# The first nine tiles' instruction list written anew in finer pieces, with 13 of 21 warming products taken out

## The chip, the cores and the metric

One core of a Trainium2 chip runs the whole kernel. The metric is device microseconds (us) of one execution; "before" has three runs: 471.3, 472.75 and 474.21, median 472.75.

## The reference

```python
# attention within chunks of 64 tokens: q, k, v are 8 x 8 x 576 x 64 (batch, heads, tokens, width)
scores = (1 / sqrt(64)) * q_c @ k_c.T
attn = exp(scores - max); attn = attn / (sum(attn) + 1e-9)
x = (attn @ v_c), heads side by side            # 4608 x 512
# SoLU feed-forward
h = x @ w_in                                    # 4608 x 1024
e = exp(h - max(h)); solu = h * e / (sum(e) + 1e-9)
ln = (solu - mean) / sqrt(var + 1e-6) * g_ln
out = ln @ w_out                                # 4608 x 512
```

The two weights arrive as 64-bit floats; the kernel reads their two 32-bit words.

## The kernel before

The 4608 tokens are 36 tiles of 128. A tile holds two chunks of 64 tokens with all eight heads. For each tile: scores (q against k), softmax, values (attn against v, the result is x transposed), the first layer into ph (128 x 1024), SoLU and normalisation into z, z turned so that its 1024 features lie on the partitions, and the second layer into po (128 x 512). The products of the two layers run in fp32r, and each operand is split into a high part and a remainder, so that three products stand for one: x_h with wi_l, x_h with wi_h, x_l with wi_h, and the same with z and wo. The first layer is 24 products of 128 x 512 (two column halves n, four row blocks cc, three pairs m), the second 24 in three thirds of eight.

TensorE (PE) does all products and some transposes. VectorE (DVE) and ScalarE (ACT) read the PSUM results. GpSimd (POOL) does small work and issues DMAs, SyncE (SP) issues most DMAs. Each engine runs its instructions strictly in the order in which the program lists them, and waits where an operand or a buffer is missing (class Order, line 40).

The work of tiles 0 to 4 and the preparation of tiles 5 to 8 stand in the string START (lines 18 to 31), word by word; each word starts a step or, if it has been begun, takes it one `yield` further (lines 750 to 768). From tile 5 on, a loop (line 775) lists the work. The words that matter here:

- n loads q and k of a tile as they lie in memory, v loads v, P loads a pair of row blocks of a weight (0 to 3 of w_in, 4 to 7 of w_out), g loads g_ln, Q and q load a batch's q and k in 32-wide strips. All of these stand in SP's queue.
- N transposes q (N:i:0) or k (N:i:1) on PE into a PSUM bank (named tp; there are two, and nat and s_e transposes, z transposes and g share them), then evicts it to qT or kT on ACT, or on DVE if the word is in MOVED (lines 34 to 37).
- c clips the high words of a weight pair (POOL, tile w_a, two buffers) and then scales them on ACT (the "prelude", w_a from w_a). b makes bits of the low words (tile w_b, DVE, or POOL if MOVED says so). C joins both on DVE. t makes the high part on ACT (wi_h or wo_h), d the remainder on DVE (wi_l or wo_l).
- S scores; A the softmax's maximum and subtraction on DVE, then the exponential on ACT; B its sum, reciprocal and product on DVE (s_e); T transposes s_e on PE and copies it to attn_t on ACT in four pieces. From tile 6 on, U turns it on DVE instead (a_b), and eight DMAs, four from SP and four from POOL, bring it to attn_t.
- V values on PE, then x_h on ACT and x_l on DVE. M first layer. X maximum (h_nmax, DVE) and exponential (ACT). Y multiplies by ph (DVE) and scales the result on ACT or POOL. R squares on ACT and a power on POOL. z turns z by PE transposes (tiles 0 and 1), Z on DVE with 16 DMAs z_t from z_b (tiles 2 and up). F one third of a second layer. o scales po into o_sb, O stores it. K turns a later tile's q and k on DVE.
- w is a product of the identity with itself into ph that nobody reads (warm, line 742); w:3 stands for three.

Of the ph tiles only tile 1's has its own PSUM place (PH2); tiles 0, 2, 3, 4 and so on follow each other in one buffer, so a tile's first product waits until DVE has multiplied the one before (Y). The loop's first values, of tiles 6 and 7, read what the eight attn_t DMAs bring. When the START list is through, the order of the loop is the same for every pair of tiles.

ffn_in (line 489) fixes the order of the 24 products; for tile 0 it sorts them by row block and yields after every six, for others it sorts by half and puts x_l last, in one piece.

Of the kernel before, what the change touches and what calls it, by code (L numbers as in the profile page):

```python
# [15 lines left out]


START = """
n:0 w:3 N:0:0 N:0:0 w:1 N:0:1 N:0:1 g w:1 S:0 A:0 G P:0 P:0 n:1 A:0 c:0 c:0 w:3 N:1:0 N:1:0 w:1
N:1:1 b:0 N:1:1 G P:1 w:1 S:1 B:0 v:0 C:0 A:1 t:0 T:0 T:0 c:1 c:1 w:4 V:0 V:0 P:2 b:1 c:2 n:2  # L20
d:0 P:3 A:1 n:3 w:6 N:2:0 w:1 N:2:1 C:1 V:0 B:1 t:1 c:2 T:1 N:2:0 b:2 N:2:1 T:1 d:1 S:2 n:4
M:0 M:0 C:2 t:2 c:3 c:3 v:1 A:2 A:2 b:3 d:2 C:3 N:3:0 N:3:1 N:3:1 M:0 N:3:0 S:3 N:4:0 B:2 N:4:1
t:3 N:4:0 A:3 P:5 d:3 c:5 N:4:1 A:3 T:2 T:2 S:4 V:1 M:0 P:4 n:5 B:3 T:3 V:1 V:1 M:1 X:0 X:0 T:3
A:4 A:4 b:4 v:2 N:5:1 c:4 n:6 P:7 c:5 N:5:0 c:4 Y:0 Y:0 n:7 N:5:1 V:2 b:5 v:3 B:4 N:5:0 V:2 b:7
C:4 z:0:1 P:6 v:5 N:6:0 X:1 v:4 C:5 N:6:0 S:5 Q:2 q:8 t:4 V:2 d:4 N:6:1 N:6:1 X:1 t:5 A:5 Y:1
M:2 z:0:1 z:0:1 X:2 A:5 R:0 z:0:0 z:0:0 q:8 N:7:1 q:8 c:6 S:6 Y:1 V:3 X:2 T:4 T:4 z:0:0 d:5 F
V:3 Y:2 Y:2 N:7:0 A:6 c:6 c:7 V:3 b:6 B:5 C:6 n:8 N:7:0 M:3 R:1 c:7 q:8 N:7:1 C:7 T:5 z:1:0 t:6
T:5 S:7 t:7 d:6 X:3 X:3 d:7 V:4 V:4 Y:3 Y:3 R:2 z:1:1 A:6 F F A:7 V:4 z:1:0 z:1:0 v:6 Z:2 A:7
M:4 F B:7 Z:3 o:0 V:5 z:1:1 z:1:1 B:6 F F v:7 O:0 X:4 N:8:0 X:4 U:6 U:7 V:5 Y:4 V:5 K:9 Y:4 N:8:0
R:4 R:3 N:8:1 N:8:1 o:1  # L30
"""


MOVED = """
N:0:0=dve N:8:0=dve N:8:1=dve Y:0=pool Y:1=pool Y:3=pool b:7=pool c:0=pool c:1=pool c:2=pool
c:3=pool c:4=pool c:5=pool c:6=pool c:7=pool
"""


# [23 lines left out]
def chunk_attention_then_solu_ffn(  # L63
# [18 lines left out]
    G = S // 32  # L82
# [24 lines left out]
    def po():  # L107
# [246 lines left out]
    def attn(i):  # L354
        return sy if order.on and i % 2 else sx
# [32 lines left out]

    def softmax_e(i):
        e = st[i, "e"]  # L390
        act.activation(e, e, AF.Exp, scale=SCALE)

    def softmax_b(i):
        e = st[i, "e"]
        ssum = small.tile([P, H], F32, name="s_sum")
        dve.tensor_reduce(out=ssum, in_=ES[i % 2], axis=AX.X, op=ALU.add)
        rinv = small.tile([P, H], F32, name="s_rinv")
        dve.reciprocal(out=rinv, in_=ssum)
        a = st[i, "e"] = work.tile([P, H, CH], F32, name="s_e") if i < PE_TURNED else e
# [66 lines left out]
        x_low(i)  # L466

    def start_softmax(i):
        softmax_a(i)
        yield  # L470
        softmax_e(i)

# [13 lines left out]
    def ffn_in(i):  # L486
        xh, xl = st[i, "x"]
        pool_h = ps_h2 if i in PH2 else ps_h
        ph = st[i, "h"] = pool_h.tile([P, 2, HALF], F32, name="ph")

        sums = [(n, cc, m) for n in range(2) for cc in range(NCC) for m in range(3)]
        if i == 0:
            sums.sort(key=lambda s: s[1])
        else:

            sums.sort(key=lambda s: (s[0], s[2] == 2))
        for at, (n, cc, m) in enumerate(sums):
            if i == 0 and at and at % 6 == 0:
                yield
            cols = slice(n * HALF, (n + 1) * HALF)  # L500
            x, w = ((xh, wi_l), (xh, wi_h), (xl, wi_h))[m]
            await_arrivals(pe.matmul(
                ph[:, n, :], x[:, cc, :], w[:, cc, cols],
                start=(cc == 0 and m == 0), stop=(cc == NCC - 1 and m == 2),
            ), at, i)
# [222 lines left out]
    first = 5  # L728
# [46 lines left out]
    for i in range(first, NT):  # L775
# [10 lines left out]
        if not odd:  # L786

            if i + 3 < NT:
                softmax_e(i + 3)
                softmax_b(i + 3)  # L790
                attn_turn(i + 3)
            if i + 1 < NT:
                x_high(i + 1)
# [17 lines left out]
        part()  # L811
        if odd:
            if i + 3 < NT:
                softmax_a(i + 3)
                softmax_e(i + 3)
            if i + 1 < NT:
                x_high(i + 1)
        elif i + 1 < NT:
            x_low(i + 1)
# [5 lines left out]
        if odd:  # L825
            if i + 1 < NT:
                x_low(i + 1)
            if i + 3 < NT:
                softmax_b(i + 3)
                attn_turn(i + 3)  # L830
        else:
            for m in (i + 4, i + 5):
                if m < NT:
                    turn(m)
# [8 lines left out]
            z_turn(i)  # L843
        store_rest()
        if odd and i + 4 < NT:
            softmax_a(i + 4)
    while queue:
        third_ahead()

# [31 lines left out]
```

## Time and profile before

| what | us |
|---|---|
| median of three runs | 472.75 |
| the profiled execution | 473.01 |
| its span, first to last instruction | 471.2 |
| PE busy | 461.9 |
| DVE busy | 374.1 |
| ACT busy | 256.4 |
| POOL busy | 147.6 |
| first product of a first layer (ph) starts | 22.39 |
| values of tile 6 start | 86.59 |

Times of rows count from the span's start. A timeline row gives start, duration, engine, line, operation, output<-input, shapes and count; in brackets stands how long the engine idled before it, and what ended that. All recorded operations have line 54, a helper, so groups are told apart by tiles and shapes. A product of 128 x 512 is shown with 0.39 us, but the next one starts 0.227 later, since they are pipelined. In windows, "x" counts records.

### The profile page before, as it was taken

The page shows a single profiled execution, that of the slowest core. Times are in us where ns is not written, and L with a number is a line of the kernel's source. Part 1 is how long each engine was busy: PE and PEld are TensorE (multiplying, and loading weights), DVE is VectorE, ACT ScalarE, POOL GpSimd, SP SyncE. Part 2 cuts the span into 40 slices and gives each one's busy share as a digit, 9 for nine tenths or more (in the row PEclk, how much of TensorE's full clock was granted, in tenths as well). Part 3 has the DMA queues.
Part 4 walks back from the last instruction along what each step waited for, and adds up shares of the span by engine and source line. Part 5 has one row for each costly group of instructions (what it writes and reads, how often), then busy time and mean ns, then how long its engine had stood idle before and what let it go on. Part 6 is the DMA issues. An engine that isn't in the chain of part 4 may idle for free.

```text
span 471.2 us, 11062 instructions
## 1 busy us (share of the span) xinstructions
PE 461.9 (98%) x4212; PEld 380.9 (81%) x4212; DVE 374.1 (79%) x521; ACT 256.4 (54%) x422; POOL 147.6 (31%) x298
## 2 busy tenths in 40 slices
PE   8999999999999999999999999999999999999997
PEld 6677778788888888888888888888888888888886
DVE  3999999797869887878788878797979797954441
ACT  2979984555544646464645455554555554545451
POOL 2212716151505050505050505042514141424430
PEclk9999999999999999999999999999999999999999
DMA  9999999878786878687258496948743535343231
GB/s 244 313 278 217 216 138 179 176 184 150 194 140 170 154 181 162 167 154 177 70 144 167 134 175 157 180 126 173 160 112 105 121 91 136 85 118 96 73 95 50
DMA packets 192924, 72.57 MB, mean 154 GB/s; under 512 B 177188, under 2 KB 177960, under 8 KB 191976
## 3 DMA queue, kind: packets, MB, share of 16 engines
q1 hardware_dynamic: 186200, 58.89, 57.3%
q0 software_dynamic: 6528, 12.86, 10.3%
q8 instruction: 33, 0.54, 0.5%
q14 instruction: 19, 0.16, 0.1%
q10 hardware_dynamic: 144, 0.13, 0.1%
HBM read 36.70 MB, written 9.44 MB: 98 GB/s over the span
## 4 chain that ended last, share of the span: by engine, by line
PE 85%; DMA 5%; DVE 3%; ACT 3%; SPq 2%; issue 1%; DVEq 0%; ACTq 0%
PE po L54 39%; PE ph L54 37%; PE tp L54 5%; PE sx L54 4%; SPq L54 2%; DMA nat<-in_q_dram 2%; DMA v_sb<-in_v_dram 2%; ACT z L54 1%; DMA attn_t<-a_b 1%; ACT attn_t L54 1%; ACT wo_h L54 1%; DVE z_b L54 1%; DVE z L54 0%; DVE s_sum L54 0%; ACT sq L54 0%
## 5 line engine op out<-in xcount | busy, mean ns | idle before, releaser
L54 ACT ACTIVATE z<-ph,h_nmax 128x1024 f32<-128x1024 f32 x36 | 40.2, 1118 | 139.1 <-DVE h_nmax L54 139.1
L54 PE MATMUL po<-wo_l,z_h 128*128 128x512 f32 (+1 forms) x288 | 113.0, 392 | 0.0
L54 PE MATMUL ph<-wi_l,x_h 128*128 128x512 f32 x288 | 112.8, 392 | 0.0
L54 PE MATMUL ph<-wi_h,x_h 128*128 128x512 f32 x288 | 112.2, 389 | 0.0
L54 PE MATMUL po<-wo_h,z_l 128*128 128x512 f32 (+1 forms) x288 | 111.6, 388 | 0.0
L54 PE MATMUL po<-wo_h,z_h 128*128 128x512 f32 (+1 forms) x288 | 111.4, 387 | 0.0
L54 POOL DMA_DIRECT2D z_t<-z_b x144 | 71.8, 506 | 27.0 <-DVE z_b L54 21.9
L54 PE MATMUL ph<-wi_h,x_l 128*128 128x512 f32 x288 | 78.1, 390 | 0.0
L54 POOL TENSOR_TENSOR u<-ssq,eps 128x1 f32<-128x1 f32 x36 | 6.8, 189 | 213.3 <-ACT sq L54 213.1
L54 DVE TENSOR_REDUCE h_nmax<-ph 128x1 f32<-128x1024 f32 x36 | 44.0, 1222 | 31.3 <-PE ph L54 31.2
L54 PEld LDWEIGHTS ph<-wi_h,x_l 128*128 128x128 f32 x288 | 53.9, 188 | 11.6 <-DVE x_l L54 0.4
L54 PEld LDWEIGHTS po<-wo_l,z_h 128*128 128x128 f32 x288 | 54.1, 188 | 11.4
L54 PEld LDWEIGHTS ph<-wi_l,x_h 128*128 128x128 f32 x288 | 54.1, 188 | 11.5 <-ACT x_h L54 0.2
L54 PEld LDWEIGHTS po<-wo_h,z_l 128*128 128x128 f32 x288 | 54.1, 188 | 11.1
L54 PEld LDWEIGHTS ph<-wi_h,x_h 128*128 128x128 f32 x288 | 54.1, 188 | 11.0
L54 PEld LDWEIGHTS po<-wo_h,z_h 128*128 128x128 f32 x288 | 54.1, 188 | 10.5
L54 DVE TENSOR_TENSOR z_l<-z_t,z_h 128x1024 fp32r<-128x1024 f32 (+1 forms) x37 | 42.0, 1136 | 20.9 <-ACT z_h L54 17.7
L54 DVE SCALAR_TENSOR_TENSOR z<-ph,z 128x1024 f32<-128x1024 f32 x36 | 44.1, 1224 | 13.3 <-ACT z L54 13.2
L54 ACT ACTIVATE z<-z,z_sum 128x1024 f32<-128x1024 f32 x33 | 38.1, 1155 | 22.9 <-DVE z L54 21.7
L54 DVE STREAM_TRANSPOSE z_b<-z 128x1024 f32<-128x1024 f32 x34 | 41.2, 1212 | 7.2 <-DMA v_sb<-in_v_dram 3.3
L54 ACT CAST z_h<-z_t 128x1024 fp32r<-128x1024 f32 (+1 forms) x37 | 36.0, 972 | 8.5 <-PE po L54 4.9
L54 ACT ACTIVATE o_sb<-po,r 128x512 f32<-128x512 f32 (+1 forms) x36 | 24.3, 674 | 24.7 <-POOL r L54 18.6
(76 smaller groups left out, 589.8 us busy)
## 6 DMA issues: line engine op xcount, KB each, us to landing
out_dram<-o_sb SPq DMA_DIRECT2D x35, 256.0 KB, 2.5
v_sb<-in_v_dram SPq DMA_DIRECT2D x32, 256.0 KB, 4.3
z_t<-z_b POOLq DMA_DIRECT2D x128, 64.0 KB, 2.8
z_t<-z_b SPq DMA_DIRECT2D x128, 64.0 KB, 3.0
q_st<-in_q_dram SPq DMA_DIRECT2D x96, 72.0 KB, 3.3
k_st<-in_k_dram SPq DMA_DIRECT2D x96, 72.0 KB, 3.1
w_raw<-in_moe_w_out_dram SPq DMA_DIRECT2D x4, 1024.0 KB, 7.5
attn_t<-a_b POOLq DMA_DIRECT2D x60, 64.0 KB, 3.8
```

Source lines behind the costliest of these rows:

```text
L54: ins = make(*args, **kwargs)
```

## The change

START lists the same work anew, MOVED sends other steps to other engines, and five functions yield in more places, so that the list can set their parts apart: the softmax's maximum, subtraction and exponential are three steps (A), its sum, reciprocal and product three (B); the two halves of a w_out pair's high part (t) and remainder (d) are two steps each; the first layer of tiles 0 to 4 comes in four pieces of six products (M). Tile 1's first layer is sorted by row block like tile 0's, and in both the two x_l products of a row block come last of its six. Warming products: 21 before (w:3 three times among them, w:4 and w:6), 8 now, all as w:1; none stands ahead of the first transposes, and five stand in a row behind the values of tile 0. The loop is as before.

```diff
 START = """
-n:0 w:3 N:0:0 N:0:0 w:1 N:0:1 N:0:1 g w:1 S:0 A:0 G P:0 P:0 n:1 A:0 c:0 c:0 w:3 N:1:0 N:1:0 w:1
+n:0 N:0:0 N:0:1 N:0:1 N:0:0 P:0 P:0 n:1 S:0 w:1 A:0 A:0 A:0 b:0 c:0 B:0 B:0 c:0 C:0 N:1:0 N:1:0
...
 MOVED = """
-N:0:0=dve N:8:0=dve N:8:1=dve Y:0=pool Y:1=pool Y:3=pool b:7=pool c:0=pool c:1=pool c:2=pool
-c:3=pool c:4=pool c:5=pool c:6=pool c:7=pool
+N:0:0=dve N:8:0=dve b:7=pool c:0=pool c:1=pool c:2=pool c:3=pool c:4=pool c:5=pool c:6=pool c:7=pool
+b:4=pool b:5=pool z:0:1=dve Y:2=pool
...
             for y in range(2):
+                if y:
+                    yield
                 g = g_sb[:, 2 * m + y:2 * m + y + 1]
                 act.activation(top[:, y], a[:, y], AF.Copy, scale=g)
...
         for y in range(2):
+            if y:
+                yield
             dve.scalar_tensor_tensor(
...
             out=nmax, in_=sv, axis=AX.X, op=ALU.max, negate=True
         )
+        yield
         e = ES[i % 2][:, :, :CH]
...
         dve.tensor_reduce(out=ssum, in_=ES[i % 2], axis=AX.X, op=ALU.add)
+        yield
         rinv = small.tile([P, H], F32, name="s_rinv")
         dve.reciprocal(out=rinv, in_=ssum)
+        yield
...
     def start_softmax(i):
-        softmax_a(i)
+        yield from softmax_a(i)
         yield
         softmax_e(i)
...
-        if i == 0:
-            sums.sort(key=lambda s: s[1])
+        if i < 2:
+            sums.sort(key=lambda s: (s[1], s[2] == 2))
         else:
             sums.sort(key=lambda s: (s[0], s[2] == 2))
         for at, (n, cc, m) in enumerate(sums):
-            if i == 0 and at and at % 6 == 0:
+            if i < first and at and at % 6 == 0:
                 yield
```

In the loop the calls of softmax_a and softmax_b become `whole(softmax_a(...))` and `whole(softmax_b(...))`, which run the parts without a break.

On POOL, from the sixth weight clip on: w_a is a clip, w_b are bits, z is a scaling of tile 0 or 1, u and r belong to tile 0's norm. Before, from the six clips of pairs 0 to 5:

```order
L54 TENSOR_SCALAR w_a<-w_raw 128x1024 x6
L54 TENSOR_SCALAR z<-z,z_sum 128x1024
L54 TENSOR_SCALAR w_b<-w_raw 128x1024
L54 TENSOR_TENSOR u<-ssq,eps 128x1
L54 TENSOR_TENSOR r<-u,mhalf 128x1
```

And now, from the clips of pairs 0 to 3 and 5:

```order
L55 TENSOR_SCALAR w_a<-w_raw 128x1024 x5
L55 TENSOR_SCALAR w_b<-w_raw 128x1024
L55 TENSOR_SCALAR w_a<-w_raw 128x1024
L55 TENSOR_SCALAR w_b<-w_raw 128x1024 x2
L55 TENSOR_SCALAR w_a<-w_raw 128x1024
L55 TENSOR_TENSOR u<-ssq,eps 128x1
```

The bits of pairs 5 and 4 have come from DVE, each behind its pair's clip; the bits of pair 7 stood on POOL before too, and pair 7's clip now comes right behind them.

On DVE, the last instructions of the list and the first of the loop: a_b turns the attention of tiles 6 (e0) and 7 (e1), the second-layer z is tile 4's. Before, from tile 4's maximum on:

```order
L54 TENSOR_REDUCE h_nmax_1076<-ph_975 128x1
L54 STREAM_TRANSPOSE a_b_1088<-e0_97 128x8x2x32
L54 STREAM_TRANSPOSE a_b_1088<-e1_98 128x8x2x32
L54 SCALAR_TENSOR_TENSOR z_1085,z_sum_1102<-ph_975,z_1085 128x1024
L54 TENSOR_TENSOR x_l_1100<-sx_96,x_h_1099 128x512
```

And now:

```order
L55 TENSOR_REDUCE h_nmax_1056<-ph_928 128x1
L55 TENSOR_REDUCE s_sum_1066<-e1_98 128x8
L55 RECIPROCAL s_rinv_1068<-s_sum_1066 128x8
L55 TENSOR_TENSOR e1_98<-e1_98,s_rinv_1068 128x8x64
L55 SCALAR_TENSOR_TENSOR z_1058,z_sum_1071<-ph_928,z_1058 128x1024
L55 COPY qT_946<-tp_948 128x512
L55 TENSOR_TENSOR x_l_1075<-sx_96,x_h_1074 128x512
L55 STREAM_TRANSPOSE a_b_1078<-e0_97 128x8x2x32
L55 STREAM_TRANSPOSE a_b_1078<-e1_98 128x8x2x32
```

Both a_b have moved behind tile 7's softmax, tile 4's multiply, an eviction of tile 8's q and tile 5's x_l.

On SP, the loads and DMAs in front of the loop: out_dram<-o_sb is tile 0's store, the v loads are those of tiles 6 and 7. Before:

```order
L54 DMA k_st<-in_k_dram 32x18x32 x8
L54 DMA v_sb<-in_v_dram 128x8x64
L54 DMA z_t<-z_b 32x512 x8
L54 DMA v_sb<-in_v_dram 128x8x64
L54 DMA out_dram<-o_sb 128x512
L54 DMA attn_t<-a_b 32x512 x4
```

And now:

```order
L55 DMA v_sb<-in_v_dram 128x8x64 x2
L55 DMA q_st<-in_q_dram 32x18x32 x8
L55 DMA k_st<-in_k_dram 32x18x32 x16
L55 DMA z_t<-z_b 32x512 x8
L55 DMA attn_t<-a_b 32x512 x4
L55 DMA out_dram<-o_sb 128x512 x2
```

The v of tile 7 has moved from behind z_t to far ahead of it, and tile 0's store from ahead of attn_t to behind it.

## Rows read from the trace of the kernel before

**Rows 1.** The page, busy time of PE and DVE in the whole span.
```profile
PE 461.9 (98%) x4212; PEld 380.9 (81%) x4212; DVE 374.1 (79%) x521; ACT 256.4 (54%) x422; POOL 147.6 (31%) x298
```
**Rows 2.** Windows: the stretch behind the first product, and the loop.
```profile
core 0: us, PE busy (x) PEld busy (x) DVE busy (x) ACT busy (x) POOL busy (x), PEclk, DMA share, GB/s
...
22.39:88.48 66.09, 63.46 (x728) 51.46 (x721) 60.96 (x86) 48.48 (x89) 24.08 (x31) 1.00 1.01 208
88.48:448.48 360.00, 360.00 (x3186) 298.13 (x3182) 292.03 (x407) 186.63 (x301) 113.58 (x244) 1.00 0.63 141
```
**Rows 3.** Timeline of PE, the first 88 us.
```profile
1.43 2.93 PE L54 MATMUL ph<-ident 128*128 128x256 f32 x6 [1.43 <-POOL e L374]
...
16.39 2.86 PE L54 MATMUL ph<-ident 128*128 128x256 f32 x12
...
22.39 0.50 PE L54 MATMUL ph<-wi_l,x_h 128*128 128x512 f32 x1
...
31.45 0.50 PE L54 MATMUL ph<-wi_l,x_h 128*128 128x512 f32 x1
...
40.42 0.69 PE L54 MATMUL sx<-attn_t,v_sb 64*64 64x64 f32 x32 [0.43 <-DMA v_sb<-in_v_dram]
...
51.37 0.48 PE L54 MATMUL po<-wo_l,z_h 128*128 128x512 f32 x1
...
62.44 0.66 PE L54 MATMUL tp<-ident,z 128*128 128x128 f32 x4 [0.67 <-ACT attn_t L54]
...
66.61 0.39 PE L54 MATMUL ph<-wi_l,x_h 128*128 128x512 f32 x1
...
79.18 0.48 PE L54 MATMUL ph<-wi_l,x_h 128*128 128x512 f32 x1
...
86.59 0.96 PE L54 MATMUL sx<-attn_t,v_sb 64*64 64x64 f32 x29 [1.09 <-DMA attn_t<-a_b]
```
**Rows 4.** The chain that ended last, one piece: start, us, what.
```profile
83.17 3.18 DMA attn_t<-a_b
```
**Rows 5.** Timeline of SP's queue, DMA issues.
```profile
1.84 0.85 SPq L54 DMA_DIRECT2D g_in<-in_moe_g_ln_dram  x1
...
75.33 0.63 SPq L54 DMA_DIRECT2D v_sb<-in_v_dram  x1
76.05 5.07 SPq L54 DMA_DIRECT2D z_t<-z_b  x8
81.22 0.53 SPq L54 DMA_DIRECT2D v_sb<-in_v_dram  x1
...
82.59 2.43 SPq L54 DMA_DIRECT2D attn_t<-a_b  x4
```
**Rows 6.** Timeline of DVE.
```profile
9.05 0.69 DVE L54 TENSOR_SCALAR w_b<-w_raw 128x1024 uint32<-128x1024 uint32 x1
...
13.59 0.69 DVE L54 TENSOR_REDUCE s_nmax<-sx 128x8 f32<-128x512 f32 x1 [0.52 <-PE sx L54]
...
30.06 1.22 DVE L54 TENSOR_TENSOR wi_l<-w_a,wi_h 128x1024 fp32r<-128x1024 f32 x1
...
65.09 1.22 DVE L54 SCALAR_TENSOR_TENSOR z<-ph,z 128x1024 f32<-128x1024 f32 x1 [0.51 <-ACT z L54]
...
72.62 0.66 DVE L54 TENSOR_TENSOR z_l<-tp,z_h 128x512 fp32r<-128x512 f32 x1
...
75.89 1.30 DVE L54 STREAM_TRANSPOSE a_b<-e 128x512 f32<-128x512 f32 x2
```
**Rows 7.** Timeline of POOL.
```profile
33.04 1.13 POOL L54 TENSOR_SCALAR w_a<-w_raw 128x1024 f32<-128x1024 f32 x1 [8.76 <-DMA w_raw<-in_moe_w_out_dram]
...
46.80 3.74 POOL L54 TENSOR_SCALAR w_b<-w_raw 128x1024 uint32<-128x1024 uint32 x1 [6.78 <-DMA w_raw<-in_moe_w_out_dram]
...
77.73 1.97 POOL L54 DMA_DIRECT2D attn_t<-a_b  x4 [0.54 <-issue]
```
**Rows 8.** Timeline of ACT, the prelude of pair 7.
```profile
57.37 1.05 ACT L54 ACTIVATE w_a<-w_a 128x1024 f32<-128x1024 f32 x1
```

More of the change, by code (lines that the diff above doesn't have):

```diff
@@ L18 @@
 START = """
-n:0 w:3 N:0:0 N:0:0 w:1 N:0:1 N:0:1 g w:1 S:0 A:0 G P:0 P:0 n:1 A:0 c:0 c:0 w:3 N:1:0 N:1:0 w:1
[L20 to L30, printed above, removed]
+n:0 N:0:0 N:0:1 N:0:1 N:0:0 P:0 P:0 n:1 S:0 w:1 A:0 A:0 A:0 b:0 c:0 B:0 B:0 c:0 C:0 N:1:0 N:1:0
@@ new lines @@
+N:1:1 g N:1:1 S:1 B:0 A:1 P:1 v:0 c:1 A:1 G G P:2 c:2 T:0 t:0 T:0 d:0 b:1 n:2 c:1 C:1 A:1 w:1 B:1
+V:0 V:0 w:1 w:1 V:0 P:3 w:1 w:1 t:1 w:1 B:1 c:3 b:2 c:2 N:2:0 B:1 C:2 N:2:1 N:2:0 w:1 T:1 N:2:1 S:2
+M:0 d:1 n:3 M:0 A:2 A:2 t:2 T:1 d:2 A:2 B:2 N:3:0 N:3:1 c:3 n:4 b:3 B:2 C:3 B:2 N:3:0 v:1 P:5 M:0
+N:3:1 S:3 A:3 A:3 N:4:0 N:4:1 t:3 N:4:0 c:5 T:2 d:3 N:4:1 V:1 b:5 S:4 A:3 M:0 B:3 B:3 V:1 T:2 B:3
+V:1 M:1 P:4 c:4 X:0 c:5 n:5 A:4 T:3 X:0 A:4 A:4 Y:0 T:3 M:1 C:5 v:2 b:4 M:1 n:6 B:4 N:5:0 M:1 X:1
+N:5:1 N:5:0 Y:0 N:5:1 V:2 v:3 v:4 V:2 z:0:1 B:4 N:6:0 z:0:1 P:7 b:7 V:2 t:5 c:7 c:4 z:0:1 n:7 M:2
@@ new lines @@
+P:6 N:6:0 X:1 S:5 B:4 R:0 A:5 N:6:1 C:4 Y:1 t:4 M:2 N:6:1 A:5 M:2 M:2 t:4 d:4 t:5 Y:1 v:5 z:0:0 d:4
+z:0:0 S:6 A:5 X:2 X:2 V:3 z:0:0 T:4 d:5 F V:3 T:4 N:7:1 c:7 M:3 N:7:1 N:7:0 N:7:0 Y:2 c:6 c:6 B:5
+B:5 d:5 V:3 M:3 B:5 A:6 Q:2 A:6 n:8 A:6 T:5 M:3 M:3 C:7 b:6 C:6 T:5 R:1 X:3 t:6 t:6 d:6 t:7 t:7 S:7
+d:6 d:7 d:7 X:3 Y:3 q:8 V:4 V:4 V:4 Y:2 z:1:1 z:1:0 F Z:2 F v:6 z:1:0 z:1:0 v:7 B:6 z:1:1 M:4 z:1:1
+M:4 o:0 B:6 N:8:0 q:8 Y:3 R:2 A:7 A:7 A:7 R:3 q:8 q:8 M:4 M:4 Z:3 B:6 F V:5 X:4 X:4 N:8:1 B:7 B:7
@@ L31 @@
+B:7 Y:4 N:8:0 V:5 V:5 U:6 U:7 F F O:0 Y:4 o:1 N:8:1 R:4 K:9
 """
 MOVED = """
-N:0:0=dve N:8:0=dve N:8:1=dve Y:0=pool Y:1=pool Y:3=pool b:7=pool c:0=pool c:1=pool c:2=pool
-c:3=pool c:4=pool c:5=pool c:6=pool c:7=pool
+N:0:0=dve N:8:0=dve b:7=pool c:0=pool c:1=pool c:2=pool c:3=pool c:4=pool c:5=pool c:6=pool c:7=pool
+b:4=pool b:5=pool z:0:1=dve Y:2=pool
 """
@@ L789, in chunk_attention_then_solu_ffn @@
                 softmax_e(i + 3)
-                softmax_b(i + 3)
+                whole(softmax_b(i + 3))
                 attn_turn(i + 3)
@@ L813, in chunk_attention_then_solu_ffn @@
             if i + 3 < NT:
-                softmax_a(i + 3)
+                whole(softmax_a(i + 3))
                 softmax_e(i + 3)
@@ L828, in chunk_attention_then_solu_ffn @@
             if i + 3 < NT:
-                softmax_b(i + 3)
+                whole(softmax_b(i + 3))
                 attn_turn(i + 3)
@@ L845, in chunk_attention_then_solu_ffn @@
         if odd and i + 4 < NT:
-            softmax_a(i + 4)
+            whole(softmax_a(i + 4))
     while queue:
```

## Prediction, made before the changed kernel was run

> **What bounds the kernel now.** I read the page first, then the windows, then the timelines of the engines up to 90 us, then the chain that ended last. The page has TensorE (PE) busy for 98% of the span and VectorE (DVE) for 79% [rows 1]. An average hides two stages, so the windows split them. From 88.48 to 448.48 PE is busy in 360.00 of 360.00 us: in the loop nothing but PE's own work sets the time, and neither the change nor any of its moved instructions is in there. From the first product at 22.39 to 88.48 it is busy in 63.46 of 66.09 us [rows 2]. So what the change can win behind 22.39 is at most the 2.63 us that PE stands idle, plus whatever lets the first products start sooner.
>
> PE's timeline says where that idle time lies [rows 3]: 0.43 at 40.42 (a v load), 0.67 at 62.44 (a transpose waits for the PSUM bank that ACT empties into attn_t) and 1.09 at 86.59, the largest. There PE is ready for the value products of tile 6 and waits for attn_t, which comes by DMA. The chain shows that DMA: issued at 83.17, 3.18 us on its way [rows 4]. SyncE's (SP) queue shows why it is issued so late: it sends v at 75.33, eight z_t pieces from 76.05 for 5.07, then another v and a store, and only at 82.59 the four attn_t pieces [rows 5], although DVE had turned tiles 6 and 7 by 75.89 + 1.30 = 77.2 [rows 6]. Ahead of 31.45 the limit is another: the fourth block of tile 0's first layer begins at 31.45 [rows 3] right behind DVE's fourth w_in remainder, 30.06 + 1.22 = 31.28 [rows 6], at the end of a DVE queue that has no gap from 13.59 on.
>
> The profiled execution took 473.01 us, of which the span is 471.2; it lies 0.26 above the median of the runs, 472.75. I add to 473.01 and take 0.26 off at the end.
>
> **The change part by part. Start to 31.45.** DVE's queue from the first join to the fourth remainder holds the same instructions as before plus g_sb and tile 0's s_e, which came earlier; else only their order differs. Before, the order left DVE 0.52 idle in front of the second tile's maximum at 13.59 [rows 6]; now s_e of tile 0 stands behind the join and fills that gap, so the maximum comes at the same time. On paper the fourth remainder ends at 31.3 again: 0. Splitting a softmax into steps costs no instruction.
>
> Thirteen warming products go. Six records (three products) took 2.93 at 1.43, and twelve took 2.86 at 16.39 [rows 3]: 0.49 against 0.24 each, so PE started at the lower of its two clocks (1.2 GHz) and ran at the upper (2.4 GHz) later, and the products themselves lay in time in which PE waited for loads and evictions. Their removal saves nothing directly. Now PE has no work at all before the first transposes, so these, the scores and the transposes of tile 1 may run at the lower clock. How long the clock then stays low no row shows. Best case: it is up by the time of tile 1's scores, 0. Worst case near the rows: everything on PE up to tile 0's attention runs at half rate; a block of 64-column products and four transposes, 0.69 and 0.66 long [rows 3], then take up to 1.35 more, which delays attn_t on ACT, the second prelude behind it and DVE's second join by about as much, and again in part at tile 2: +2.0. I take +0.5, since the eight products left come as five in a row just ahead of tile 2. On the other side, g_in is issued behind tile 1's loads, and w_in's first pair 0.85 us sooner [rows 5]; the DMA engines are full by then, so I count 0, and -0.85 as the bound.
>
> **31.45 to tile 5's first layer (79.18).** The set of PE's instructions is the same: 47.73 us before. Old waits: 0.43 and 0.67 [rows 3]. New ones, from queues laid out with the durations of the rows:
> - Bits of pairs 4 and 5 leave DVE (0.69 each [rows 6]) for POOL, where the one such row lasts 3.74 [rows 7]. POOL takes pair 5's clip (33.04 + 1.13 = 34.2), its bits (to 37.9), pair 4's clip (39.1) and bits (42.8). So join 5 can start at 38.0 and join 4 at 43.0; their w_out halves are needed by the first po product, 51.37 before [rows 3]. Hidden: DVE and ACT need some 5 us behind 43.0 for both halves, which leaves about 2.
> - ph has one buffer for tiles 2 to 5, so tile 3's first product waits for tile 2's multiply on DVE and tile 4's for tile 3's. The latter multiply stood at 65.09 [rows 6]; I get 64.7, and PE, 1.4 us ahead there without the bank wait of 62.44, now waits about 0.7 for it: tile 4 starts at 65.9 instead of 66.61 [rows 3]. Tile 3 waits 0.4 likewise.
> - Tile 8's first transposes stand inside tile 4's first layer and need the bank that z_l of tile 1 frees. That z_l stood at 72.62 [rows 6] and hurt nobody; now it comes at about 69.4, behind z_b of tile 2 and a sum, and PE would be there at 68.6: +0.9.
> Gains and new waits cancel: tile 5 starts at 79.1 + 0.5 = 79.6.
> - DVE loses 2 x 0.69 and N:8:1, gains z:0:1; ACT takes three of z's scalings from POOL and gives it one. Both have room where PE does not wait for them; what remains of it is in the waits above.
>
> The Trainium skill (GPSIMD Engine Reference, 4.1 Engine selection) has one-input element work at roughly line rate on GpSimd. The clip agrees, 1.13 for 1024 columns; the bits, with 3.74 on 32-bit integers, do not [rows 7], so the measurement decides. By the rule POOL would be 2 x 2.6 us sooner with pair 4, and the sum would not change, since that is hidden either way.
>
> **The wait at 86.59.** Before, PE was ready for tile 6's values at 86.59 - 1.09 = 85.50; now, 0.4 later, at 85.9. attn_t's DMAs: a_b of tiles 6 and 7 is moved behind tile 4's multiply, tile 8's eviction and x_l, and ends at 79.2 instead of 77.2. POOL's four pieces went out at 77.73 in 1.97 [rows 7]; now at 79.3 to 81.3. SP's come last: v of tile 7 (0.53) now stands ahead of z_t, and the store behind attn_t. So z_t runs about 76.6 to 81.7, and attn_t goes out at 81.8, not 82.59. With the landing of 3.18 [rows 4] the wait ends 0.8 sooner; if the extra v, 256 KB at the 208 GB/s of this stretch [rows 2], holds SP back for 1.2 us and not 0.53, 0.2 sooner. I take 0.5: 86.1, just behind PE's 85.9. Losses further up cost nothing as long as PE is ready before that.
>
> **Sum.** Start +0.5, middle -0.1, both inside the wait; wait -0.5; loop 0. 473.01 - 0.5 - 0.26 = 472.25, said as 472.3.
>
> **Rivals.**
> (a) *The clock stays low into the products* (slower). For: without warmers PE idles between small bursts. Against: five products remain in a row ahead of tile 2. Place: 22.39 to 31.45, 9.06 us in which PE is busy for some 8.7, by the 96% of the stretch [rows 2]; at half rate +8.7, less the 1.1 of the wait at 86.59 and 0.5 of slack before 31.45: about +7.1, 479.9. It decides from the point where the granted clock is low beyond tile 0's second block. The Trainium skill (TensorE: Matmul & The Clock Gate, Part 1) says the low clock is the default and returns when PE idles; the rows at 1.43 and 16.39 agree on the two rates, and no row shows a fall.
> (b) *ACT stands at pair 7's prelude* (slower, little). Three v loads (512 KB) now go ahead of w_out's pair 7, whose bits began on POOL at 46.80 [rows 7]: 2.5 us later at 208 GB/s, then 3.74 and 1.13: the prelude starts at 54.2 (pair 6's came first before, pair 7's at 57.37 [rows 8]). Each us beyond that holds the evictions, attn_t and the exponentials queued behind it on ACT, and so tile 4. With 4 us more, about +3, less the wait: +2, 474.5. For: POOL's bits are the slowest row of the start. Against: at the rate of the stretch the prelude comes no later than pair 7's did before.
> (c) *All waits go* (faster): 2.63 of idle and 0.85 at the start, 469.3. For: finer steps put each result nearer to its use. Against: ph's single buffer and SP's queue, which finer steps don't touch.
> (d) *Nothing moves PE*: the DMA wait ends where it did, 472.7.
>
> **How the numbers follow.** Forecast 0.52 (own range 471.3 to 473.7), (d) 0.15, (b) 0.13, (c) 0.12, (a) 0.08. One per cent, 4.7 us, is about what a measurement of this kernel can tell from no change; its three runs spread over 2.9 us. Only (a), and the worst of (b), pass it upward: 0.09. Downward 3.5 us are all there is, so only an error in this reading does: 0.04. The rest, 0.87, is the same. The range goes to (c)'s inner half and past (b): 470.0 to 475.8.
>
> **What would show it.** Right: the first product at 21.5 to 23, the fourth block of tile 0 at 31.3 to 32.5, tile 5 at 79 to 80, attn_t from SP at about 81.8, the values of tile 6 at about 86.1, and from there the same 384.6 us to the end. Half-rate records of 0.2 us between transposes at 4 to 16 us would show the start's cost; the same among ph products means (a). An idle ACT in front of a w_a prelude around 54 us and tile 4 later than 66.6 means (b). The forecast is wrong if tile 6's values start outside 85 to 88.

## The result and the profile after

The changed kernel takes 476.16 us (median of seven runs, 473.03 to 477.81); the kernel before took 472.72 beside it (seven runs, 471.3 to 474.21). The ratio is 1.0079 [1.0055, 1.0102]: slower by 3.4 us, under one per cent, where 472.3 and a range up to 475.8 had been forecast. The profiled execution took 476.14, its span is 474.4; before it was 473.01 and 471.2.

The windows behind the first product and of the loop, changed kernel, answer to [rows 2]:

```profile
core 0: us, PE busy (x) PEld busy (x) DVE busy (x) ACT busy (x) POOL busy (x), PEclk, DMA share, GB/s
26.75:91.63 64.88, 63.67 (x727) 50.72 (x721) 61.80 (x84) 51.36 (x93) 29.07 (x30) 1.00 0.93 209
91.63:451.63 360.00, 360.00 (x3186) 298.13 (x3182) 291.56 (x406) 185.72 (x301) 113.59 (x244) 1.00 0.64 141
```

The loop is untouched: 360.00 of 360.00, and it starts 91.63 - 88.48 = 3.15 late. The stretch ahead of it is 64.88 long, with 1.21 of idle time in it, where it was 66.09 with 2.63. So the loss lies ahead of the first product: 26.75 instead of 22.39, 4.36 late. PE's timeline, changed kernel, answers to [rows 3]:

```profile
4.21 1.08 PE L55 MATMUL tp<-ident,nat 128*128 128x128 f32 x4 [4.21 <-DMA nat<-in_q_dram]
...
7.34 1.14 PE L55 MATMUL sx<-kT,qT 64*64 64x64 f32 x32 [0.68 <-ACT kT L55]
...
18.06 6.34 PE L55 MATMUL ph<-ident 128*128 128x256 f32 x10
24.20 1.11 PE L55 MATMUL tp<-ident,nat 128*128 128x128 f32 x8
...
26.75 0.50 PE L55 MATMUL ph<-wi_l,x_h 128*128 128x512 f32 x1
...
35.65 0.50 PE L55 MATMUL ph<-wi_l,x_h 128*128 128x512 f32 x1
...
56.55 0.50 PE L55 MATMUL po<-wo_l,z_h 128*128 128x512 f32 x1 [0.19 <-DVE wo_l L55]
...
69.29 0.50 PE L55 MATMUL po<-wo_l,z_h 128*128 128x512 f32 x1 [0.41 <-DVE wo_l L55]
...
71.19 0.47 PE L55 MATMUL ph<-wi_l,x_h 128*128 128x512 f32 x1 [0.24 <-DVE z L55]
...
83.91 0.39 PE L55 MATMUL ph<-wi_l,x_h 128*128 128x512 f32 x1
...
91.63 0.50 PE L55 MATMUL po<-wo_l,z_h 128*128 128x512 f32 x1
```

Three things are to be seen. Blocks of scores take 1.14 instead of 0.69: PE is at 1.2 GHz, and it stays there until about 24 us, where the transposes behind the row at 18.06 are short again. (The rate is read from the length of the records here. The column PEclk gives 1.00 for 4.21 to 24.20 as well, as it does for the first 5 us before, where six records took 2.93: up to the first rise it doesn't show the lower clock.) The row at 18.06 is five warming products (ten records); at the upper clock six of them took 2.86 [rows 3], here five take 6.34. And the old waits are gone: nothing at 40, at 62, or ahead of tile 6's values, with 0.19, 0.41 and 0.24 in their place.

The chain that ended last, changed kernel (start, us, what), runs through that row piece by piece:

```profile
18.13 1.16 PE ph L55 x2
...
19.34 1.24 PE ph L55 x2
...
20.62 1.24 PE ph L55 x2
...
21.90 1.24 PE ph L55 x2
...
23.18 1.22 PE ph L55 x2
```

Each warming product draws a ph tile of its own from the one buffer, so each waits for the one before and starts up to 1.28 behind it. A product is two records, and at this clock a record without such a wait took 0.49 (2.93 for six) [rows 3], so some 0.98 of the 1.28 is its own work. Behind the row stand tile 2's transposes. From there the chain stays on PE, but for one eviction (qT), up to tile 0's fourth block; its last piece ahead of that block and the block's first:

```profile
34.63 1.09 PE sx L55 x64
35.72 3.08 PE ph L55 x12
```

DVE, which has no gap from 13.59 on before [rows 6], now stands too:

```profile
26.89 0.69 DVE L55 TENSOR_REDUCE s_nmax<-sx 128x8 f32<-128x512 f32 x1 [2.46 <-PE sx L55]
...
34.05 1.22 DVE L55 TENSOR_TENSOR wi_l<-w_a,wi_h 128x1024 fp32r<-128x1024 f32 x1
```

It idles 2.46 for tile 2's scores, and the fourth w_in remainder starts at 34.05 instead of 30.06. It ends at 35.27, ahead of the fourth block at 35.65 (31.45 before), and PE goes into that block without a wait: what is late there is PE's own queue.

### The profile page after: what moved, and what is told of

The parts are those of the page before. It is cut to its first block, busy times and chain, and to the rows that moved or that the text cites. A ratio compares the mean times of both kernels' runs of the same rounds, so it can differ in the third digit from the quotient of the medians.

```text
span 474.4 us, 11012 instructions
## 1 busy us (share of the span) xinstructions
PE 463.3 (98%) x4186; PEld 378.9 (80%) x4186; DVE 375.2 (79%) x519; ACT 258.4 (54%) x424; POOL 152.7 (32%) x298
## 4 chain that ended last, share of the span: by engine, by line
PE 92%; DVE 5%; DMA 1%; SPq 1%; issue 0%; ACT 0%; DVEq 0%; ACTq 0%
PE ph L55 41%; PE po L55 41%; PE tp L55 6%; PE sx L55 5%; DMA nat<-in_q_dram 1%; DVE wo_l L55 1%; DVE w_a L55 1%; SPq L55 1%; DVE z L55 1%; DVE h_nmax L55 0%; DVE s_e L55 0%; DVE e L55 0%; DVE x_l L55 0%; DVE z_l L55 0%; DVE z_h L55 0%
## 5 line engine op out<-in xcount | busy, mean ns | idle before, releaser
L55 ACT ACTIVATE z<-z,z_sum 128x1024 f32<-128x1024 f32 x35 | 40.3, 1153 | 23.0 <-DVE z L55 21.9
```

Source lines behind the costliest of these rows:

```text
L55: ins = make(*args, **kwargs)
```

## The experiments

Theory 1: the five single warming products, which PE meets at the lower clock, hold its queue while tile 2's data lies ready. Rival A: the lower clock costs it, and the five are what ends it. Rival B: the new order costs it. "First product", "fourth block" and "loop" are the starts of tile 0's first and fourth block and of the loop's first output product in each kernel's one profiled execution; medians and ratios are of all its runs, the ratio against runs of before taken beside them:

| kernel | first product | fourth block | loop | median us | ratio |
|---|---|---|---|---|---|
| before | 22.39 | 31.45 | 88.48 | 472.72 | 1 |
| changed | 26.75 | 35.65 | 91.63 | 476.16 | 1.0079 [1.0055, 1.0102] |
| e1 without the five | 23.21 | 32.49 | 88.31 | 473.6 | 1.0024 [1.001, 1.0038] |
| e2 all 21 back | 22.33 | 31.38 | 87.80 | 472.24 | 0.9999 [0.9983, 1.0014] |
| e3 first three back | 28.02 | 36.91 | 92.57 | 476.71 | 1.0087 [1.0068, 1.0105] |
| e4 the five in one tile | 23.78 | 32.81 | 88.67 | 473.17 | 1.003 [1.0016, 1.0044] |
| e5 old order, new eight | 26.91 | 35.80 | 91.20 | 475.79 | 1.0073 [1.0045, 1.01] |
| e6 first five back, row out | 22.21 | 31.16 | 87.23 | 472.74 | 1.0011 [0.9998, 1.0024] |
| e12 first five back, row kept | 22.28 | 31.17 | 87.09 | 475.68 | 1.0049 [1.0026, 1.0073] |

**e1: the row of five out.**

```diff
-V:0 V:0 w:1 w:1 V:0 P:3 w:1 w:1 t:1 w:1 B:1
+V:0 V:0 V:0 P:3 t:1 B:1
```

> The changed kernel without the five warming products that stand in a row behind tile 0's values and ahead of tile 2's transposes; everything else as changed. Theory 1 (these five, each at half rate and each waiting for the one before, hold PE's in-order queue for 6.3 us while tile 2's data lies ready): the transposes of tile 2 start at 18.1 to 19.6 instead of 24.20, the first product at 22.5 to 23.6 instead of 26.73, tile 0's fourth block at 31.3 to 32.5 instead of 35.63, and the time is 472.5 to 474. Rival A (they are what raises the clock; without them the products start at the lower clock): the first products come early but take twice as long each, fourth block 36 or later, time 477 to 482. Rival B (the new order itself costs the time behind 31 us): time stays at 475.5 to 476.5 although the first product is early.

Measured 473.6: 2.6 of the 3.4 us come back, and rival A falls. PE's timeline of e1:

```profile
18.32 2.12 PE L55 MATMUL tp<-ident,nat 128*128 128x128 f32 x8 [0.55 <-DMA nat<-in_q_dram]
20.23 1.06 PE L55 MATMUL ph<-ident 128*128 128x256 f32 x2
...
22.59 0.69 PE L55 MATMUL sx<-kT,qT 64*64 64x64 f32 x32
23.21 0.50 PE L55 MATMUL ph<-wi_l,x_h 128*128 128x512 f32 x1
```

Tile 2's data is there at 18.3, and it waited until 24.20 in the changed kernel. The clock rises by 22.59 without the row too. So of the 4.36 that the first product lost, the row accounts for 26.75 - 23.21 = 3.54; the 0.82 that are left come with the transposes, 2.12 long at the lower clock. By the loop this execution has made them up (88.31), but it is the fastest of ten, 0.8 under their median: where the 1.4 us of the median against its own before (472.21) lie, no profile shows.

**e2: all 21 warming products at their old places, in the new order.**

```diff
-n:0 N:0:0 N:0:1
+n:0 w:3 N:0:0 w:1 N:0:1
...
-V:0 V:0 w:1 w:1 V:0 P:3 w:1 w:1 t:1 w:1 B:1 c:3 b:2 c:2 N:2:0
+w:4 V:0 V:0 V:0 P:3 t:1 B:1 c:3 b:2 c:2 w:6 N:2:0
```

> The changed kernel with all 21 warming products back at the places they had before (three ahead of the first transpose, then one, one, three, one, one, four, six, one); the new order of all other steps stays. Theory 1 (the missing products keep PE at the lower clock up to 24 us): tile 0's scores take 0.69 again instead of 1.14, the twelve records ahead of tile 2 take 2.9 instead of 6.3 for ten, first product 22.2 to 23.2, fourth block 31.2 to 32.2, time 472 to 473.6. Rival A (clock): the same, 472 to 473.6. Rival B (the new order costs it): 475 to 476.5 with the first product early. If the waits that the new order removes (0.67 at 62.44 and 1.09 at 86.59 before) stay away and nothing is late in their place: down to 470.5.

Measured 472.24, the time of before. Rival B falls: the order alone costs nothing, and wins nothing. PE's timeline of e2 shows why:

```profile
7.39 0.69 PE L55 MATMUL sx<-kT,qT 64*64 64x64 f32 x32 [0.24 <-ACT kT L55]
...
16.10 2.86 PE L55 MATMUL ph<-ident 128*128 128x256 f32 x12
...
63.45 0.50 PE L55 MATMUL po<-wo_l,z_h 128*128 128x512 f32 x1 [0.58 <-DVE wo_l L55]
...
66.01 0.47 PE L55 MATMUL ph<-wi_l,x_h 128*128 128x512 f32 x1 [0.20 <-DVE z L55]
...
85.36 0.30 PE L55 MATMUL sx<-attn_t,v_sb 64*64 64x64 f32 x2 [0.43 <-DMA attn_t<-a_b]
...
86.25 0.63 PE L55 MATMUL sx<-attn_t,v_sb 64*64 64x64 f32 x27 [0.60 <-DMA attn_t<-a_b]
```

The waits of 0.43 and 0.67 [rows 3] gave way to 0.58 and 0.20, and the DMA wait ends at 86.25 where it ended at 86.59.

**e3: w:3 ahead of the first transpose, nothing else.**

```diff
-n:0 N:0:0 N:0:1
+n:0 w:3 N:0:0 N:0:1
```

> The changed kernel with three warming products ahead of the first transpose and nothing else; the five in a row stay. If three records' worth of work at the very start are enough to raise the clock and it then holds: scores 0.69, five warming products 2.4 to 3.5 us instead of 6.3, first product about 22.5 to 23.5, time 472.5 to 474. If the clock falls again or never rises with only these: scores 1.14, five at 1.2 to 1.3 us each, first product 26.5 to 27, time 475.5 to 476.5 (theory 1 then needs the products between as well). Rival B: 475.5 to 476.5 even with the first product early.

Measured 476.71: three products at the start don't keep the clock up. In the profiled execution the scores of tile 0 and the row are at half rate; in the other three runs the mean granted clock is 0.981, so it rose and fell again (the mean leaves out the time ahead of the first rise: the changed kernel's is 0.999 or 1):

```profile
1.42 2.93 PE L55 MATMUL ph<-ident 128*128 128x256 f32 x6 [1.42 <-POOL ident masks.py:199]
...
6.94 1.14 PE L55 MATMUL sx<-kT,qT 64*64 64x64 f32 x32 [0.67 <-ACT kT L55]
...
17.73 6.34 PE L55 MATMUL ph<-ident 128*128 128x256 f32 x10
```

**e5: the order of before, with the changed kernel's eight warming products.**

```diff
-n:0 w:3 N:0:0 N:0:0 w:1 N:0:1 N:0:1 g w:1 S:0
+n:0 N:0:0 N:0:0 N:0:1 N:0:1 g S:0
...
-w:6 N:2:0 w:1 N:2:1
+w:1 w:1 w:1 w:1 w:1 N:2:0 N:2:1
```

> The kernel before with its order of all steps, but with the changed kernel's eight warming products at the changed kernel's places (one ahead of tile 1's transposes, one ahead of tile 0's values, five single ones ahead of tile 2's transposes, one ahead of tile 1's attention transposes) in place of its 21. Theory 1 (warming products alone cause the late start): scores of tile 0 about 1.14, the five about 6.3 us, first product 26 to 27.5 instead of 22.39, time 475 to 477.5, at or above the changed kernel's. Rival B (the order causes it): first product within 1 us of 22.39 and time 472 to 473.5.

Measured 475.79, 0.4 under the changed kernel, with the row again 6.34 long. With e2 this closes the square: old or new order, the time goes with the warming products.

**e4: the row as one word, w:5, so that the five share a tile.**

```diff
-V:0 V:0 w:1 w:1 V:0 P:3 w:1 w:1 t:1 w:1 B:1
+V:0 V:0 w:5 V:0 P:3 t:1 B:1
```

> The changed kernel with its five single warming products in a row drawn as five products into one tile; nothing else. If a part of their 6.3 us is that each waits for the end of the one before, because each has a tile of its own in one buffer: ten records at 0.49 us each, 4.9 us, so tile 2's transposes start 1.4 us sooner (about 22.8), the first product at 25.3, fourth block 34.2, time 475 to 475.6 (ratio 1.005 to 1.0065). If the row without waits also raises the clock while it runs, the rest of it goes at 0.24: 3 to 4 us, first product 24 to 25, time 474 to 475. If the lower clock is all: still 6.3 us, 476.2.

Measured 473.17, 3.0 less than the changed kernel for the same products at the same place, and below every case expected. Windows of PE's records of ph, e4 (length, busy time and records, PEclk, DMA share, GB/s):

```profile
18.01:20.12 2.11, 2.11 (x5) 1.00 1.15 342
20.12:21.46 1.34, 1.34 (x6) 1.00 0.97 357
```

Without waits between them the products take 3.45 instead of 6.34, and from 20.12 on a record takes half as long: the row that doesn't wait is also past the lower clock 4 us sooner. The row now costs the first product 23.78 - 23.21 = 0.57 and not 3.54. How much of the difference is the waits themselves and how much the sooner rise, this run doesn't part.

**e6 and e12: the first five of before back, without and with the row of five.**

```diff
-n:0 N:0:0 N:0:1 N:0:1 N:0:0 P:0 P:0 n:1 S:0
+n:0 w:3 N:0:0 w:1 N:0:1 N:0:1 N:0:0 P:0 P:0 n:1 w:1 S:0
```

> The changed kernel with the first five of the 21 warming products back at their old places (three ahead of the first transpose, one between its two sets of transposes, one ahead of tile 0's scores) and the five in a row ahead of tile 2 taken out; three single ones stay as changed. If the clock, once up at about 6 us, holds over PE's waits of up to 1 us between 8 and 19 us: scores 0.69 throughout, first product 22.2 to 23, fourth block 31.3 to 32.2, time 472 to 473. If it falls again without the four and six ahead of tile 2: scores of tile 1 at 1.1 and the time as without the five alone, 473.2 to 474, or worse, with the products at half rate, 475 to 480.

> The changed kernel, all its eight warming products where they are (the five single ones in a row too), with the first five of before added (three ahead of the first transpose, one between its two sets, one ahead of tile 0's scores). If the row of five costs only because it finds PE at the lower clock: the clock is up by 8 us and stays, the five take 2.6 to 3.3 us instead of 6.34 and end before tile 2's data (18 to 19.4), first product 22.1 to 22.8, fourth block 31.1 to 32.0, time 472 to 473 (ratio 0.9995 to 1.0015). If five single products cost by standing in the queue at either clock: first product 24 or later, 473.5 to 475.

e6 measured 472.74. Its clock rises and then falls once more, as its windows and the rows of PE at the fall show:

```profile
7.62:17.86 10.24, 6.07 (x115) 4.17 (x114) 8.81 (x13) 7.27 (x12) 3.29 (x3) 1.00 1.18 324
17.86:21.28 3.42, 3.19 (x13) 2.55 (x14) 3.42 (x7) 3.10 (x5) 1.17 (x1) 0.50 1.00 345
```

```profile
15.35 1.07 PE L55 MATMUL sx<-attn_t,v_sb 64*64 64x64 f32 x30 [0.27 <-ACT attn_t L55]
18.09 2.10 PE L55 MATMUL tp<-ident,nat 128*128 128x128 f32 x8 [1.68 <-DVE w_a L55]
```

PE had been busy for 6.07 of 10.24 us and had just stood for 1.68 when the granted clock fell to 0.50. All ten runs show a fall (mean granted clock 0.986 to 0.996); with no row of products on PE there its ratio is 1.0011, inside 0.9998 to 1.0024. e2's ten runs all lie at 0.999 or 1.

e12 is the sharpest of the runs, because its clock goes both ways with one program. In four of twelve runs the mean granted clock is 0.999 or 1, and they took 471.59, 472.35, 472.45 and 472.61; in the other eight it is 0.984 to 0.989, and they took 475.04 to 476.83. The profiled execution is one of the four; its row of five:

```profile
16.23 3.73 PE L55 MATMUL ph<-ident 128*128 128x256 f32 x10
```

The medians of the two groups are 472.40 and 475.87, 3.5 us apart. e6 is the same program without the row, its clock fell in all ten runs, and it is 0.1% slower than before. So the five single products cost nothing at the upper clock; the lower clock costs little without them (0.1% in e6, 0.2% in e1, whose profile shows it up to some 22 us); and most of the loss comes where the row meets the lower clock. The ratio in the table, 1.0049, is of both groups together. My expectation had taken it for granted that the first five hold the clock; in eight of twelve runs they don't. That the eight runs stood at the lower clock during the row is inferred from their mean clock and times; none of them was profiled. An estimate of how long it lasted: e6's profiled 0.996 goes with the 3.42 us at 0.50 above, and by the same working 0.985 of 474 us is some 14 us.

**e10: e2 with the bits of pairs 4 and 5 back on DVE.**

```diff
-b:4=pool b:5=pool z:0:1=dve Y:2=pool
+z:0:1=dve Y:2=pool
```

> The changed kernel with all 21 warming products and the bits of pairs 4 and 5 back on DVE, 0.69 each, where POOL takes 3.74 and 3.73. If POOL's long rows are what makes wo_l late at 63.45 (0.58) and z at 66.01 (0.20): both waits go, tile 4 starts at 65.0 to 65.4 instead of 66.01, and the wait for attn_t behind it grows by what was won, so the time stays at 471.9 to 472.5. If the wait comes from ACT's and DVE's own queues: 0.5 to 0.7 stays at 63.45, and DVE's 1.4 us of added work make it or another wait longer, 472.2 to 473.2.

Measured 473.58, ratio 1.0033 [1.002, 1.0047]. The wait for wo_l stays (0.41), so POOL's long rows don't make it alone. In e2 and e10 alike DVE starts on these remainders right behind the first of ACT's four wo_h pieces (61.10 behind 60.36, 63.83 behind 63.06), and the pieces stand behind tile 1's squares in ACT's queue; in e8, below, the squares are moved and the wait is gone. A new wait comes, PE's and DVE's timelines of e10:

```profile
36.45 0.73 PE L55 MATMUL ph<-wi_h,x_l 128*128 128x512 f32 x2 [1.97 <-DVE x_l L55]
```

```profile
33.54 0.69 DVE L55 TENSOR_SCALAR w_b<-w_raw 128x1024 uint32<-128x1024 uint32 x1 [2.01 <-DMA w_raw<-in_moe_w_out_dram]
```

At this place of the new list the bits wait for their load, and on DVE they hold up x_l of tile 1. That the row on POOL is five times as long doesn't matter there, since POOL has nothing else to do at that time.

**e7, e8, e9, e11: the wait for attn_t.** e7 is e2 with all eight pieces from POOL and SP's z_t ahead of the last four k_st loads; e8 is e7 with R:1 behind t:7; e9 is e2 with SP's four pieces on ACT's queue; e11 is before with those four on ACT and U:6 U:7 behind V:5.

The line in e7 and e8, and the one in e9 and e11:

```diff
-                        arriving[i // 2].append((pool if x == y else sync).dma_start(
+                        arriving[i // 2].append((pool if x == y or i < 8 else sync).dma_start(
```

```diff
-                        arriving[i // 2].append((pool if x == y else sync).dma_start(
+                        arriving[i // 2].append((pool if x == y else act if i < 8 else sync).dma_start(
```

> The changed kernel with all 21 warming products (472.24) and two edits behind 70 us: all eight attn_t pieces of tiles 6 and 7 go out from POOL's queue instead of four from SP's, and SP sends z_t of tiles 2 and 3 ahead of the last four k_st loads. If SP's late attn_t is what PE waits for at 85.4 and 86.3 (0.43 and 0.60): both waits shrink to under 0.3, attn_t issued by 83.5, the loop's first output product at 86.8 to 87.3 instead of 87.80, time 471.2 to 471.9 (ratio 0.998 to 0.9995). If something else holds the loop's start (z_t's landing, DVE's z_l): the waits go, the output product still starts at 87.6 to 87.9, time 472 to 472.6.

> As the run before it, and tile 1's squares (eps, sq on ACT; the root on POOL) behind the four wo_h pieces instead of ahead of them. If ACT's 1.5 us there is what makes PE wait for wo_l at 63.45 (0.58): that wait falls to 0.0 to 0.2, tile 4 starts at 65.4 to 65.7 instead of 66.01, and with the wait for attn_t gone the loop starts 0.3 to 0.5 sooner again: 470.8 to 471.5. If POOL's root of tile 1 now holds z of tile 2 up: a new wait for z_b or z_t, 472 or more.

> The changed kernel with all 21 warming products (472.24, ratio 0.9999) and one edit: the four attn_t pieces of tiles 6 and 7 that SP sent at 82.31, behind eight z_t pieces, go out from ACT's queue as soon as DVE has turned them (a_b ends at 78.75). If SP's queue alone makes PE wait at 85.36 and 86.25 (0.43 and 0.60): pieces out by 81 and landed by 85, both waits gone or under 0.2, the loop's first output product at 86.9 to 87.3 instead of 87.80, time 471.3 to 472.0, ratio 0.997 to 0.9995. If the loads that SP now sends 2.4 us sooner delay the pieces as they did where all eight went by POOL: a wait of 1 to 3 us at the same place, 472.5 to 475.

> The kernel before with one edit of the same kind: tile 6's and 7's a_b behind tile 4's multiply and x_l of tile 5 on DVE, and SP's four attn_t pieces on ACT's queue from there. If the wait of 1.09 at 86.59 is worth its length: gone or under 0.2, loop starts at 87.4 to 87.8 instead of 88.48, time 471.2 to 471.9, ratio 0.9975 to 0.999. If the loads sent sooner take it back: ratio 0.9995 to 1.005.

All four are slower than before: 1.0082 [1.0065, 1.0099], 1.0124 [1.0096, 1.0153], 1.0055 [1.0035, 1.0076] and 1.0072 [1.0048, 1.0095]. In e7 POOL has sent the last piece by 80.47 + 3.91 = 84.38, but SP, free sooner, has by then begun the next batch; POOL's and SP's queues and PE's timeline, e7:

```profile
80.47 3.91 POOL L55 DMA_DIRECT2D attn_t<-a_b  x8 [1.60 <-PE po L55]
```

```profile
83.78 7.56 SPq L55 DMA_DIRECT2D q_st<-in_q_dram  x9
```

```profile
89.66 1.02 PE L55 MATMUL sx<-attn_t,v_sb 64*64 64x64 f32 x27 [3.44 <-DMA attn_t<-a_b]
...
93.02 0.63 PE L55 MATMUL po<-wo_h,z_h 128*128 128x512 f32 x1
```

The pieces take up to 5.7 us to land, where e2's take up to 3.6 and its loads begin at 86.45. e8 agrees (loads from 83.22, up to 5.5), and so does e11 (88.36, 2.9); that the loads are what slows the pieces is read from this order, no run shows it by itself. The wait grows to 3.44, and during it the clock falls: PEclk is 0.50 from 88.36 to 95.19, and a product of 0.39 takes 0.63. (This profiled execution, 478.43, is the slowest of its four.) In e11 the wait for attn_t is gone, and PE waits for z_h instead. ACT, in order, stands until DVE has turned the pieces and then issues them for 2.52 us, so its next scaling starts 4.6 later than before (83.21 against 78.58) and z_h 2.5 later (87.31 against 84.80); ACT's and PE's timelines, e11:

```profile
80.64 2.52 ACTq L54 DMA_DIRECT2D attn_t<-a_b  x4
83.21 1.15 ACT L54 ACTIVATE z<-z,z_sum 128x1024 f32<-128x1024 f32 x1 [5.20 <-DMA attn_t<-a_b]
```

```profile
88.39 0.50 PE L54 MATMUL po<-wo_l,z_h 128*128 128x512 f32 x1 [1.10 <-ACT z_h L54]
...
89.65 0.50 PE L54 MATMUL po<-wo_h,z_l 128*128 128x512 f32 x1 [0.53 <-DVE z_l L54]
```

e8 does away with the wait for wo_l and makes one of 1.53 for z at tile 4: the squares now stand ahead of tile 3's exponential on ACT, which starts at 64.77 instead of e7's 64.15, and tile 4 starts at 67.39, e7's at 67.18. e9 shortens the wait for attn_t to 0.44, yet its profiled execution is 1.4 late at tile 4 already (67.40 against 66.01), ahead of the edit, and e7's is 1.2 late there. Of e9's 1.4, some 0.45 lie ahead of the first product (22.78 against 22.33), and most of the rest where DVE's queue differs. DVE's timelines, e2 and then e9, with POOL's of e9:

```profile
47.14 1.41 DVE L55 SCALAR_TENSOR_TENSOR wo_l<-w_a,g_sb,wo_h 128x512 fp32r<-128x512 f32 x2
```

```profile
47.79 2.36 DVE L55 SCALAR_TENSOR_TENSOR wo_l<-w_a,g_sb,wo_h 128x512 fp32r<-128x512 f32 x2
```

```profile
48.45 3.74 POOL L55 TENSOR_SCALAR w_b<-w_raw 128x1024 uint32<-128x1024 uint32 x1 [3.86 <-DMA w_raw<-in_moe_w_out_dram]
```

The same two remainders take 2.36 instead of 1.41, and POOL's bits begin 0.66 into them; z_l stands behind them on DVE, and PE waits 0.42 for it at 51.94, which e2 doesn't. e7 and e8 show the same (2.29 and 2.32, waits of 0.36 and 0.47). So a part of what these three profiled executions lose is not the edit's; why e9 is slower in its median stays open beyond that. No kernel of this study beats the one before.

## Why the prediction was wrong

**The start (+0.5, bounds -0.85 and +2.0; measured +4.2 at the fourth block): this step failed.** It saw that PE would run at the lower clock, and priced scores and transposes at half rate. What it left out is the rest of the row: it took "the eight products left come as five in a row just ahead of tile 2" for help with the clock and counted their own time at nothing, as if they still lay in PE's spare time. Spare time was a property of the upper clock: before, six products in 2.86 fitted ahead of tile 2's data; at the lower clock, and each waiting for the one before, five did not. The row behind those six, before:

```profile
19.43 0.66 PE L54 MATMUL tp<-ident,nat 128*128 128x128 f32 x4 [0.19 <-DMA nat<-in_q_dram]
```

What the runs showed in its place: 3.54 of the 4.36 at the first product are the row (e1), 0.82 the rest at half rate, which the +0.5 had about right. The bound of +2.0 was drawn from the nearest rows of other operations, while the price of the warming products themselves at half rate stood in [rows 3]: 2.93 for six records, so 4.9 for ten where 2.4 would have done, +2.5 more; 2.0 and 2.5 together are near the 4.2. The rest of the 6.34 is the wait of each product for the one before, which no term held. The prediction also followed the start on DVE's queue, and took the fourth block at 31.45 to hang on the remainder that ends at 31.28. No row shows PE waiting for that remainder, before or after; the path was PE's queue.

**The reading of the clock.** The forecast "how long the clock then stays low no row shows" was honest, but the choice of +0.5 went to the lower end. Rival (a) had the right mechanism and the wrong place: the clock does not stay low into the products, it is up ahead of them (tile 2's scores, at 26.13, take 0.69). Its 479.9 is as far off as the forecast. The Trainium skill (TensorE: Matmul & The Clock Gate, Part 1) says that the number of matmuls at the low clock varies from run to run of one kernel. e12's four and eight runs fit that, though what varies there is whether the clock falls a second time. The Trainium skill, in the same part, calls the cost of the ramp, for modelling, under one per cent of a typical span. Here the low clock and the row together cost 0.8% (476.16 against e2's 472.24), all of the effect there was to forecast.

**The middle (-0.1; measured +0.5 from the fourth block to tile 5, 48.26 against 47.73).** In e2, where the start is as before, it is 78.70 - 31.38 = 47.32, -0.4. The waits at 40.42 and 62.44 went as forecast; wo_l came in their place, where I had expected ph and z_l: POOL's bits took 4.04, 4.59 and 3.71, but with two of them back on DVE the wait stayed (e10). Tile 3's and tile 8's waits did not appear; tile 4's did, 0.24 of the 0.7. The prediction's own terms, tile 4 0.7 sooner and then +0.9, make +0.2 and not -0.1; that moves its sum by 0.1 at most.

What sets the changed kernel's +0.5 apart from e2's -0.4 is 0.94 in one stretch, from tile 0's first output product to tile 3's first product: 54.50 to 57.79, where e2 has 50.15 to 52.50. There the products with wo_l start at 54.50, 55.50 and 56.55, where e2 has 50.15, 50.93 and 51.62, and the last of them waits for DVE. DVE's timeline of the changed kernel, POOL's, and DVE's of e2:

```profile
55.03 1.47 DVE L55 SCALAR_TENSOR_TENSOR wo_l<-w_a,g_sb,wo_h 128x512 fp32r<-128x512 f32 x1
```

```profile
54.83 1.12 POOL L55 TENSOR_SCALAR w_a<-w_raw 128x1024 f32<-128x1024 f32 x1
```

```profile
50.20 0.74 DVE L55 SCALAR_TENSOR_TENSOR wo_l<-w_a,g_sb,wo_h 128x512 fp32r<-128x512 f32 x1
```

The remainder takes twice as long where a clip of POOL begins 0.20 ahead of it. e1 and e4 have the same pair of rows (1.47 each). Whether the clip is the cause no run shows.

**The wait at 86.59 (-0.5; given back -1.6).** With the loss of the start PE comes too late for attn_t to matter, and the stretch from tile 5's first product to the loop is 7.72 long instead of 9.30; 1.09 of that is the wait. Sum: 4.2 + 0.5 - 1.6 = 3.1, the 3.15 of the loop's start. In e2, where PE comes in time, the wait ends at 86.25 against the forecast 86.1. That end was right; on the way to it SP sent the pieces at 82.31 and not at 81.8, and they landed sooner than in 3.18 (a median of 2.1), so two errors cancelled.

**Rivals.** (d), nothing moves PE, is what the order alone does (e2, 0.9999). (c), all waits go, holds for the old waits only. (b) did not come about: tile 4 waits for z and wo_l, not for a prelude. (Its "three v loads" are two that are new ahead of pair 7, as its 512 KB say.) The range ended 0.36 below the result, since it took in half of (c) and little of any slower case, and none with the row in it.

## What to carry to other kernels

Before a filler instruction is called free, price it at the clock, and with the buffer, that it will meet: an in-order queue makes it work on the path as soon as its cover is gone. If products are there to raise the clock, draw them into one tile, so that none waits for another (3.45 instead of 6.34 us here), and see over many runs that the clock holds. A queue that is freed sooner sends its next loads sooner, and what one wanted early may then land later (up to 5.7 us in e7, 3.6 in e2).

## What was not expected of the hardware

One and the same program (e12) held the clock in four of twelve runs and lost it in eight, and the two groups differ by 2.4 to 5.2 us. The clock fell in e6 behind a wait of 1.68, having held through one of 1.40 at 12.50, and in e7 during one of 3.44; in the kernel before it held through the 1.09 at 86.59. In the changed kernel it stayed low from 4.21 to about 24.2, although PE was busy in 17.63 of those 19.99 us and never stood for more than 0.68.

DVE's remainders of wo_l take 1.40 or 1.41 for two in six profiled executions (before, e2, e3, e6, e10, e12). In the other eight two of them take 1.76 to 2.36, and each time a clip or bits on POOL begin at most 0.6 us ahead of them or while they run. It is no rule yet: in e12 the bits begin at 47.81, between the start of the two (46.94) and their end, and these keep 1.41 while the bits take 4.13 instead of 3.73. Whether one causes the other was not tried.
